# From head 16 on, two pieces of a pair's attention scores stand back to back on TensorE

## The chip, the core and the metric

The kernel runs on one core of a Trainium2 chip. The metric is the time of one execution in device microseconds (us); a measured figure is the median over several runs. A trace of one profiled execution stands beside it. The engines are called by the names of the profile: PE is TensorE, DVE is VectorE, ACT is ScalarE, POOL is GpSimd, SP is SyncE, which issues the transfers. PEld is PE's loading of weights. PSUM is the memory with eight banks into which PE writes.

## What is computed

Attention over 8 batches of 8 heads, 576 positions, 64 numbers per head, with a mask in blocks of 64; then a dense layer with a low-rank mixing over positions and two large matrices; then a gated layer. All in 32-bit floats.

```python
scores = scale * np.matmul(q, k.transpose(0, 1, 3, 2))
scores = np.where(mask, scores, -1000000000.0)          # block_i >= block_j
attn = softmax(scores); x = np.matmul(attn, v)          # (8, 576, 512)
...
u = x + (x.transpose(0, 2, 1) @ U @ V).transpose(0, 2, 1)
x = u + np.maximum(u @ w_ch1, 0.0) @ w_ch2
...
out = (sigmoid(conv(x, conv_w)) * (x @ w_val)) @ w_out
```

## The kernel before

The 8 x 576 positions are cut into nine groups of 512. For each group and each of 16 slices of the large layer, `emit_h1` sums twelve matmuls into one PSUM bank (tile `h1`, written at line 833; the trace calls it `h`), ACT makes `hh` of it and DVE makes `hl` (lines 861, 862), and `emit_o` adds twelve matmuls to the four accumulators `acc` (line 885). This is the main stream on PE. The accumulators hold four of the eight PSUM banks for the whole time.

The attention of later heads is woven into that stream. `attention` is a generator; `gap()` is called in the middle and at the end of every `emit_h1` and `emit_o`, and pulls about one step of the generator each time. So a step of the attention falls in one of four kinds of place: in the middle of an `h1` sum, after it, in the middle of an `o` sum, after it. In `tick(n, ...)`, four steps of head n come first, i = 0 to 3. From head 16 on (`n >= NQ`), an even head does the scores of itself and the next head there: `emit_s_piece(n // 2, i)` computes piece i of both, one head in each half of PE's rows, into two fresh PSUM banks (tiles `pS`, matmuls at line 381), and ACT copies the two banks out (line 386). Piece 0 has three blocks of 64, 192 and 256 columns per head, piece 1 one of 320, piece 2 one of 448, piece 3 one of 320. [...] There are 24 pairs of heads from head 16 on.

The two `pS` tiles of a piece, `h1`, and the tiles `pPV` (attention times values, line 604), `pT`, `pG` and `pH` (mixing) all come from one pool of four banks, `ps_p`. A bank is free again when its last reader is done: for `h1` that is `hl` on DVE, for `pS` the copy on ACT, for `pPV` the copy `lt` on ACT (line 606).

PE's order is written out by hand: its instructions stand as the code emits them. The order of the other engines is set by a scheduler when the program is built, so it can move when PE's order does.

Of the kernel before, what the change touches and what calls it, by code (L numbers as in the profile page):

```python
# [22 lines left out]
def attn_moe_gate_kernel(ctx: ExitStack, tc: tile.TileContext, q, k, v, U, V, w1, w2, wval, convw, wout, out):  # L23
# [303 lines left out]
    def load_v(n):  # L327
        if not 0 <= n < NH:
            return
        vv = v[n // H, n % H]  # L330
        t = vstk[n % 2]
        sp.dma_start(out=t[:, 0:NK - 1, 0:D], in_=vv[0:S - D, :].rearrange("(i p) d -> p i d", p=P))
        sp.dma_start(out=t[D:P, NK - 1, 0:D], in_=vv[S - D:S, :])
# [4 lines left out]
    def spare(nm, n):  # L338
        return st_p.tile([P, n], F32, tag=nm, name=nm)
# [4 lines left out]
    def prep_t(pn):  # L344
        if pn >= B * NP:
            return
        t = raw.pop(pn)
        if 2 * pn < NQ:
            tq = rot("tk" if pn % 2 else "tq", 1)
            z = kz[pn % 2]  # L350
            for rows in own if pn == 0 else (slice(0, P),):
                vec.transpose(tq[rows], t["q"][rows])
                for a in range(2):
                    if pn or rows == own[a]:
                        vec.transpose(z[own[a], a, :], t["k"][own[a]])
            qkt[pn] = (tq, z)
        else:
            tq, tk = rot("tq", 1), rot("tk", 1)
            vec.transpose(tq, t["q"])
            vec.transpose(tk, t["k"])  # L360
            qkt[pn] = (tq, tk)
        load_qk(pn + 1)

    def kslice(j):
        return slice(q0[j], q0[j] + P) if q0[j] + P <= S else slice(S - P, S)
# [3 lines left out]
    def emit_s_piece(pn, i):  # L369

        heads = (2 * pn, 2 * pn + 1)
        tq, tk = qkt[pn]
        if i == 0:
            for n in heads:
                stt[n] = [spare(("za", "zb")[h], w) if n % 3 == 1 else s_p.tile([P, w], F32, tag=f"s{h}", name=f"s{h}") for h, w in enumerate(sw)]
        ps = [psum["a"].tile([P, 512], F32, tag="a", name="pS") for _ in own]
        o = 0
        for j, a0, a1 in pieces[i]:
            w = a1 - a0
            for t, me in zip(ps, own):  # L380
                pe.matmul(t[:, o:o + w], tk[me, kslice(j)], tq[me, a0:a1], start=True, stop=True)  # L381
            o += w
        j, a0, a1 = pieces[i][0]
        d = soff[j] + a0 - q0[j]
        for n, t in zip(heads, ps):
            act.copy(stt[n][half_of[j]][:, d:d + o], t[:, 0:o])  # L386
# [72 lines left out]
    def emit_corners(n):  # L459
        for h, js in enumerate(((3, 0), (1, 2))):  # L460
            c0, c1 = (soff[j] // D for j in js)
            v_ = stt[n][h].rearrange("p (c w) -> p c w", w=D)
            pool.memset(v_[D:P, c0:c1 + 1:c1 - c0, :], MASKED)
        pool.memset(sv(n, NK - 1)[0:D], MASKED)
# [7 lines left out]
    def emit_max_a(n):  # L472
        m = rot("m", 1)
        vec.tensor_tensor(m[:, P:], sv(n, 0, P), sv(n, 1), op=ALU.max)
        for j in range(2, NK):
            x = vec.tensor_tensor(m[:, q0[j]:], m[:, q0[j]:], sv(n, j), op=ALU.max)
        noted(1, x)
        mxt[n] = m

    def emit_max_b(n):  # L480
        m = mxt.pop(n)
        t = rot("t")
        vec.transpose(t[:, 0:P], sv(n, 0)[:, 0:P])
        vec.transpose(t[:, P:], m[:, P:])
        r = tiny_p.tile([P, NB32], F32, tag="r0", name="r0")
        vec.reduce_max(r, t.rearrange("p (j a) -> p j a", a=32), axis=AX.X)
        mxt[n] = r

    def emit_max_c(n):
        r = mxt.pop(n)  # L490
        r2 = tiny_p.tile([P, NB32], F32, tag="r1", name="r1")
        vec.tensor_copy(r2[0:64], r[64:128])
        yield
        vec.tensor_tensor(r[0:64], r[0:64], r2[0:64], op=ALU.max)
        yield
        vec.tensor_copy(r2[0:32], r[32:64])
        yield
        vec.tensor_tensor(r[0:32], r[0:32], r2[0:32], op=ALU.max)
        yield
        vec.tensor_copy(r[32:64], r[0:32])  # L500
        yield
        vec.tensor_copy(r[64:128], r[0:64])
        yield
        mb = rot("mb", 1)
        vec.transpose(mb.rearrange("p (j a) -> p j a", a=32), r.rearrange("p (j o) -> p j o", o=1).to_broadcast([P, NB32, 32]))
        mbt[n] = mb


    def emit_sub(n, half):
        mb = mbt[n]  # L510
        for j in parts[half]:
            noted(3, vec.tensor_tensor(sv(n, j), sv(n, j), mb[:, q0[j]:], op=ALU.subtract))  # L512
# [3 lines left out]
    def prep_v(n):  # L516

        if not FIRST_SPLIT <= n < NH:
            return
        t = vstk[n % 2]  # L520
        vlo[n] = late["v"].tile([P, NK, D], F32R, tag="vlo", name="vlo")
        if not vhi:
            vhi[0] = late["v"].tile([P, NK, P], F32R, tag="vhi", name="vhi")
            act.copy(vhi[0][:, :, D:P], t[:, :, D:P])
        v_, h_ = t[:, :, 0:D], vhi[0][:, :, 0:D]
        hi_act(h_, v_)
        lo(pool, vlo[n], v_, h_)
# [3 lines left out]
    def emit_exp(n):  # L531
        if n < FIRST_SPLIT:
            return
        for half in range(2):
            s = stt[n][half][:, 0 if half else WHOLE:]
            act.activation(s, s, AF.Exp, scale=scale)  # L536
# [73 lines left out]
    def emit_norm_a(pn):  # L610
        lt = lts.pop(pn)
        t = rot("t")
        with behind(NR0 if pn < NP else 0):
            vec.transpose(t, lt)
        r = tiny_p.tile([P, NB32], F32, tag="r0", name="r0")
        vec.tensor_scalar(r, t.rearrange("p (j a) -> p j a", a=32)[:, :, 0], 1e-9, None, op0=ALU.add)
        vec.reciprocal(r, r)
        nrm[pn] = r

    def emit_norm_b(pn):  # L620
        xt, r = xts[pn], nrm.pop(pn)
        rb = rot("t")
        vec.transpose(rb.rearrange("p (j a) -> p j a", a=32), r.rearrange("p (j o) -> p j o", o=1).to_broadcast([P, NB32, 32]))
        pool.tensor_tensor(xt, xt, rb, op=ALU.mult)
# [90 lines left out]
    def tick(n, mixed, last=B * NP):  # L715


        e = n - DEPTH
        new, old = n < NH, 0 <= e < NH

        load_v(e + 1)
        for i in range(4):
            if n < NQ:
                with tc.high_priority():
                    emit_q_bank(n, i)
            elif new and n % 2 == 0:
                emit_s_piece(n // 2, i)
            if i == (0 if n % 2 else 3) and new and n >= NQ:
                emit_corners(n)
                emit_max_a(n)  # L730
            yield
        if new:
            if n >= NQ:
                emit_max_b(n)
            if n % 2 == 1:
                prep_t((n + 1) // 2)
        yield from mixing(2 * e, mixed, last)
        if new and n >= NQ:
            for _ in emit_max_c(n):
                pass  # L740
            emit_sub(n, 0)
            emit_sub(n, 1)
        if old:
            emit_pv(e, 0)
            yield
        if new and n >= NQ:
            emit_exp(n)
        if old:
            emit_pv(e, 1)
        prep_v(e + 1)  # L750
        emit_est(e + 1)
        if old:
            if e % 2 == 1:
                with tc.high_priority() if URG and e == H - 1 else ExitStack():
                    emit_norm_a(e // 2)
                    emit_norm_b(e // 2)
            yield
        yield from mixing(2 * e + 1, mixed, last)

    def mixing(at, first, last=B * NP):  # L760

        for step, delay in ((mix_H2, H0), (mix_G, G0), (mix_T, T0)) if last == NP else ((mix_H2, HPOS), (mix_G, GPOS), (mix_T, TPOS)):
            pn, off = divmod(at - delay, 4)
            if off == 0 and first <= pn < last:
                if URG and pn == NP - 1:
                    with tc.high_priority():
                        for _ in step(pn):
                            pass
                else:
                    yield from step(pn)  # L770
                yield step is mix_H2 and pn % NP == NP - 1
# [391 lines left out]
```

## Time and profile before

| | |
|---|---|
| median of 3 runs | 1480.73 us (1478.81 to 1481.48) |
| span of the profiled execution, first to last instruction | 1473.3 us |
| PE busy / ACT busy / DVE busy | 1426.3 us (97%) / 718.5 us (49%) / 1054.8 us (72%) |
| chain that ended last, PE's share | 82% |
| matmuls of the score pieces (line 381) | 576 rows, from 218.6 to 1005.6 us |

A busy engine is one with an instruction in it; matmuls overlap, so PE's pace is read from the distance between the starts of two matmuls, not from their durations. The profiled span and the measured median differ by 7.4 us; that part lies around the span and has no instructions of the kernel.

### The profile page before, as it was taken

What the parts mean: (1) busy time and instruction counts of PE and PEld (TensorE: products, weight loads), DVE (VectorE), ACT (ScalarE), POOL (GpSimd) and SP (SyncE); (2) the same over time, 40 slices, a digit from 0 to 9 for tenths busy, and PEclk for the clock granted to TensorE, in tenths of its full rate; (3) what the DMA queues carried; (4) which work ended last, traced back from release to release, by engine and by line L of the source; (5) the groups of instructions that cost most, each with busy time, mean ns of one, the idle gap of its engine ahead of it and who ended that gap; (6) DMA issues with size and microseconds to landing.
All of it is one profiled execution on the core that took longest, in us unless ns stands there. A gap on an engine that the chain in (4) does not pass through costs nothing.

```text
span 1473.3 us, 20082 instructions
## 1 busy us (share of the span) xinstructions
PE 1426.3 (97%) x6706; PEld 1102.3 (75%) x6706; DVE 1054.8 (72%) x2224; ACT 718.5 (49%) x1529; POOL 297.8 (20%) x420
## 2 busy tenths in 40 slices
PE   6888899899999999999999999999999999999999
PEld 3656666677777777777777777777888888788887
DVE  7878877967786888777778878777224326399991
ACT  4676564555555546565555555555322221344332
POOL 2113332212121112112211211121122100343310
PEclk9999999999999999999999999999999999999999
DMA  6445764543343434333434433332255433223311
GB/s 123 104 106 154 217 210 130 152 110 96 84 102 110 95 96 111 96 86 82 124 82 111 114 83 96 96 95 70 86 159 167 147 128 123 92 72 101 109 56 65
DMA packets 246288, 163.56 MB, mean 111 GB/s; under 512 B 197669, under 2 KB 212261, under 8 KB 246186
## 3 DMA queue, kind: packets, MB, share of 16 engines
q1 hardware_dynamic: 246186, 162.29, 39.6%
q8 instruction: 53, 0.87, 0.3%
q14 instruction: 49, 0.40, 0.1%
HBM read 134.98 MB, written 27.26 MB: 110 GB/s over the span
## 4 chain that ended last, share of the span: by engine, by line
PE 82%; DVE 10%; DMA 3%; ACT 2%; issue 1%; SPq 1%; POOL 0%; DVEq 0%; ACTq 0%
PE acc L885 25%; PE h L833 25%; PE pPV L604 8%; PE o L999 7%; PE val L975 6%; PE pS L381 6%; DMA raw<-in_moe_w_ch_dram 1%; DVE wa L123 1%; DVE rq L425 1%; PE pG L680 1%; PE acc L878 1%; PE pS L416 1%; DVE wa L141 1%; PE pT L664 1%; DVE wa L120 1%
## 5 line engine op out<-in xcount | busy, mean ns | idle before, releaser
L885 PE MATMUL acc<-hh,w 128*128 128x512 f32 x1152 | 401.0, 402 | 0.0
L885 PEld LDWEIGHTS acc<-hh,w 128*128 128x128 f32 x1152 | 217.1, 188 | 67.6 <-issue 22.5
L833 PE MATMUL h<-uh,w1hi 128*128 128x512 f32 x576 | 238.5, 414 | 2.3 <-ACT lt L606 1.2
L833 PE MATMUL h<-uh,w1lo 128*128 128x512 f32 x576 | 226.4, 393 | 0.0
L885 PE MATMUL acc<-hl,w 128*128 128x512 f32 x576 | 225.9, 392 | 0.0
L833 PE MATMUL h<-ul,w1hi 128*128 128x512 f32 x576 | 225.7, 392 | 0.0
L862 DVE SCALAR_TENSOR_TENSOR hl<-h,hh 128x512 fp32r<-128x512 f32 x144 | 98.5, 684 | 143.2 <-ACT hh L861 142.0
L861 ACT ACTIVATE hh<-h 128x512 fp32r<-128x512 f32 x144 | 85.9, 596 | 173.9 <-PE h L833 167.9
L833 PEld LDWEIGHTS h<-uh,w1hi 128*128 128x128 f32 x576 | 108.6, 189 | 45.7 <-issue 20.4
L95 POOL TENSOR_TENSOR vlo<-vstk,vhi 128x320 fp32r<-128x320 f32 x46 | 43.0, 934 | 455.3 <-ACT vhi L89 389.2
L833 PEld LDWEIGHTS h<-uh,w1lo 128*128 128x128 f32 x576 | 108.4, 188 | 24.2
L885 PEld LDWEIGHTS acc<-hl,w 128*128 128x128 f32 x576 | 108.8, 189 | 19.8 <-issue 0.7
L833 PEld LDWEIGHTS h<-ul,w1hi 128*128 128x128 f32 x576 | 108.7, 189 | 19.6 <-issue 1.3
L957 DVE SCALAR_TENSOR_TENSOR gt<-yb,cw,gt 128x516 f32<-128x516 f32 (+1 forms) x144 | 115.2, 830 | 1.4
L381 PE MATMUL pS<-tq,tk 64*128 64x320 f32 (+4 forms) x576 | 96.7, 429 | 1.5 <-DVE hl L862 0.8
L95 POOL TENSOR_TENSOR yl<-yb,yh 128x512 fp32r<-128x512 f32 (+7 forms) x64 | 66.9, 1078 | 107.4 <-ACT yh L89 107.3
L386 ACT COPY s<-pS 128x320 f32<-128x320 f32 (+2 forms) x128 | 60.2, 497 | 48.7 <-PE pS L381 47.5
L95 POOL TENSOR_TENSOR ul<-xt,uh 128x512 fp32r<-128x512 f32 (+7 forms) x64 | 53.8, 850 | 108.0 <-ACT uh L89 107.9
L536 ACT ACTIVATE s<-s 128x448 f32<-128x448 f32 (+1 forms) x62 | 44.0, 710 | 64.8 <-DVE s L512 64.8
L381 PEld LDWEIGHTS pS<-tq,tk 64*128 64x128 f32 x576 | 43.8, 185 | 37.8 <-issue 22.2
L512 DVE TENSOR_TENSOR s<-s,mb 128x64 f32<-128x64 f32 (+4 forms) x160 | 68.7, 493 | 0.3
L605 ACT COPY xt<-pPV 64x128 f32<-64x128 f32 (+1 forms) x128 | 50.1, 391 | 25.8 <-PE pPV L604 23.9
(169 smaller groups left out, 2758.8 us busy)
## 6 DMA issues: line engine op xcount, KB each, us to landing
w<-w_s SPq DMA_DIRECT2D x144, 512.0 KB, 3.3
rawq<-in_q_dram SPq DMA_DIRECT2D x128, 72.0 KB, 2.8
rawk<-in_k_dram SPq DMA_DIRECT2D x128, 72.0 KB, 3.1
out_dram<-ot SPq DMA_DIRECT2D x35, 256.0 KB, 2.0
vstk<-in_v_dram SPq DMA_DIRECT2D x64, 128.0 KB, 2.7
raw<-in_moe_w_ch_dram SPq DMA_DIRECT2D x64, 128.0 KB, 2.8
raw<-in_moe_w_ch_dram SPq DMA_DIRECT2D x16, 512.0 KB, 3.9
w_s<-wo SPq DMA_DIRECT2D x16, 512.0 KB, 3.3
```

Of the source, the lines that this page charges most:

```text
L95: eng.tensor_tensor(o, i, f32(h), op=ALU.subtract)
L381: pe.matmul(t[:, o:o + w], tk[me, kslice(j)], tq[me, a0:a1], start=True, stop=True)
L386: act.copy(stt[n][half_of[j]][:, d:d + o], t[:, 0:o])
L512: noted(3, vec.tensor_tensor(sv(n, j), sv(n, j), mb[:, q0[j]:], op=ALU.subtract))
L604: pe.matmul(o_, l_, r_, start=(i == 0), stop=(i == len(todo) - 1))
L833: pe.matmul(ps[:, 0:n], w[:, d, fs], x[:, d, 0:n], start=(d == 0 and i == 0), stop=(d == ND - 1 and i == 2))
L861: act.activation(hh[:, 0:n], ps[:, 0:n], AF.Relu)
L862: latest[0] = vec.scalar_tensor_tensor(hl[:, 0:n], ps[:, 0:n], 0.0, f32(hh[:, 0:n]), op0=ALU.max, op1=ALU.subtract)
L885: pe.matmul(acc[d][:, 0:n], w[:, wi, ds], x[:, 0:n], start=False, stop=(f == NF - 1 and i == 2))
L957: vec.scalar_tensor_tensor(gt[d][:, 0:gw], y[:, d, j:j + gw], cw[:, d, j:j + 1], gt[d][:, 0:gw], op0=ALU.mult, op1=ALU.add)
L975: pe.matmul(ps[:, 0:n], w[:, d, es], x[:, d, 0:n], start=(i == 0), stop=(i == 3 * ND - 1))
L999: pe.matmul(ps[:m, cs], x[:, e, a:a + m], w[:, e, cs], start=(i == 0), stop=(i == 3 * ND - 1))
```

## The change

Two lines in `tick`. Steps i = 0 and i = 2 now emit two pieces each, steps 1 and 3 none; the yields stay, so nothing else moves to another step.

```diff
-            elif new and n % 2 == 0:
+            elif new and n % 2 == 0 and i % 2 == 0:
                 emit_s_piece(n // 2, i)
+                emit_s_piece(n // 2, i + 1)
```

On PE in the middle of an `h1` sum, before (the last block of piece 0, half of the sum, piece 1; `w` and `u` names are weights and inputs, numbers are buffers; the bracket names the engines waited for):

```order
L381 MATMUL pS_4344<-tq_4244,tk_4245 128x256
L381 MATMUL pS_4345<-tq_4244,tk_4245 128x256
L833 MATMUL h1_4331<-uh_757,w1hi_148 128x512
L833 MATMUL h1_4331<-ul_758,w1hi_148 128x512
L833 MATMUL h1_4331<-uh_757,w1lo_149 128x512
L833 MATMUL h1_4331<-uh_757,w1hi_148 128x512
L833 MATMUL h1_4331<-ul_758,w1hi_148 128x512
L833 MATMUL h1_4331<-uh_757,w1lo_149 128x512
L381 MATMUL pS_4364<-tq_4244,tk_4245 128x320 [waits PE_49,Activation_49]
L381 MATMUL pS_4365<-tq_4244,tk_4245 128x320 [waits Activation_49]
```

The same place now (lines below 727 of the new file stand one further down):

```order
L381 MATMUL pS_4344<-tq_4244,tk_4245 128x256
L381 MATMUL pS_4345<-tq_4244,tk_4245 128x256
L381 MATMUL pS_4354<-tq_4244,tk_4245 128x320 [waits PE_49,Activation_49]
L381 MATMUL pS_4355<-tq_4244,tk_4245 128x320 [waits Activation_49]
L834 MATMUL h1_4331<-uh_757,w1hi_148 128x512
L834 MATMUL h1_4331<-ul_758,w1hi_148 128x512
L834 MATMUL h1_4331<-uh_757,w1lo_149 128x512
```

Piece 1 moved ahead of the second half of the sum. `h1` holds a bank here; the built program gives the four `pS` tiles banks 6, 7, 4 and 6 again.

On PE after an `h1` sum, before (end of piece 0, half of an `o` sum, piece 1):

```order
L381 MATMUL pS_4023<-tq_3918,tk_3919 128x256
L885 MATMUL acc0_3225<-hh_3895,w2_3899 128x512 [waits DMAHW4_49]
L885 MATMUL acc0_3225<-hl_3896,w2_3899 128x512
L885 MATMUL acc0_3225<-hh_3895,w2_3899 128x512
L885 MATMUL acc1_3226<-hh_3895,w2_3899 128x512
L885 MATMUL acc1_3226<-hl_3896,w2_3899 128x512
L885 MATMUL acc1_3226<-hh_3895,w2_3899 128x512
L381 MATMUL pS_4040<-tq_3918,tk_3919 128x320 [waits PE_49,Activation_49]
L381 MATMUL pS_4041<-tq_3918,tk_3919 128x320 [waits Activation_49]
```

And now:

```order
L381 MATMUL pS_4023<-tq_3918,tk_3919 128x256
L381 MATMUL pS_4032<-tq_3918,tk_3919 128x320 [waits PE_49,Activation_49]
L381 MATMUL pS_4033<-tq_3918,tk_3919 128x320 [waits DVE_49]
L886 MATMUL acc0_3225<-hh_3895,w2_3899 128x512 [waits DMAHW4_49]
L886 MATMUL acc0_3225<-hl_3896,w2_3899 128x512
```

The fourth tile now takes the bank of the sum just finished and waits for DVE's `hl`.

On ACT at one of the six places where a group of positions ends, before (copies of `pPV`, casts `eh`, exponentials at lines 536 and 556):

```order
L89 CAST eh_7287<-za_6768 128x448
L89 CAST eh_7291<-zb_6769 128x768
L556 ACTIVATE ef_7285<-za_6768 128x384
L605 COPY xt_7260<-pPV_7268 64x448
L606 COPY lt_7261<-pPV_7268 64x448
L89 CAST vhi_2942<-vstk1_153 128x5x64
L536 ACTIVATE s0_7088<-s0_7088 128x448
L536 ACTIVATE s1_7089<-s1_7089 128x768
```

And now:

```order
L89 CAST eh_7287<-za_6768 128x448
L536 ACTIVATE s0_7088<-s0_7088 128x448
L89 CAST eh_7291<-zb_6769 128x768
L556 ACTIVATE ef_7285<-za_6768 128x384
L536 ACTIVATE s1_7089<-s1_7089 128x768
L605 COPY xt_7260<-pPV_7268 64x448
L606 COPY lt_7261<-pPV_7268 64x448
```

Both exponentials of line 536 moved ahead of the copies `xt` and `lt`; the next `pT` (line 672) waits for `lt`.

## Rows read from the trace of the kernel before

**Rows 1.** Windows: stretch, its length, then busy us by engine, granted clock, DMA.

```profile
300.00:1012.00 712.00, 711.08 (x3500) 547.35 (x3499) 555.83 (x1234) 392.16 (x833) 129.93 (x237) 1.00 0.38 98
```

**Rows 2.** Waits of PE, 300 to 1012 us: total, times, longest.

```profile
PE pT L672 <- ACT lt L606: 0.9, 2, 0.7
```

**Rows 3.** Timeline of PE (start, length, instruction, count): pieces 0 and 1 apart.

```profile
425.22 0.39 PE L833 MATMUL h<-uh,w1lo 128*128 128x512 f32 x1
425.54 1.25 PE L381 MATMUL pS<-tq,tk 64*128 64x64 f32 x12
426.72 0.50 PE L833 MATMUL h<-uh,w1hi 128*128 128x512 f32 x1
427.06 0.40 PE L833 MATMUL h<-ul,w1hi 128*128 128x512 f32 x1
...
428.01 0.39 PE L833 MATMUL h<-uh,w1lo 128*128 128x512 f32 x1
428.32 0.81 PE L381 MATMUL pS<-tq,tk 64*128 64x320 f32 x4
429.06 0.50 PE L885 MATMUL acc<-hh,w 128*128 128x512 f32 x1
429.40 0.39 PE L885 MATMUL acc<-hl,w 128*128 128x512 f32 x1
429.63 0.62 PE L885 MATMUL acc<-hh,w 128*128 128x512 f32 x2
```

**Rows 4.** Timeline of PEld, weight loads in the same stretch.

```profile
426.72 0.19 PEld L833 LDWEIGHTS h<-uh,w1hi 128*128 128x128 f32 x1 [0.33 <-issue]
...
427.06 0.19 PEld L833 LDWEIGHTS h<-uh,w1lo 128*128 128x128 f32 x1
```

**Rows 5.** Timelines where pieces 0 and 1 already adjoin: PE, PEld, DVE, ACT.

```profile
292.56 2.28 PE L381 MATMUL pS<-tq,tk 64*128 64x64 f32 x16
294.77 0.50 PE L885 MATMUL acc<-hh,w 128*128 128x512 f32 x1
...
293.43 0.64 PE L381 MATMUL pS<-tq,tk 64*128 64x256 f32 x3
293.64 0.70 PE L381 MATMUL pS<-tq,tk 64*128 64x320 f32 x2
294.04 0.29 PEld L381 LDWEIGHTS pS<-tq,tk 64*128 64x128 f32 x2 [0.21 <-DVE hl L862]
293.29 0.69 DVE L862 SCALAR_TENSOR_TENSOR hl<-h,hh 128x512 fp32r<-128x512 f32 x1
293.84 1.73 ACT L386 COPY s<-pS 128x512 f32<-128x512 f32 x4 [0.58 <-PE pS L381]
```

**Rows 6.** ACT by form, 300 to 1012 us: busy us, mean ns, idle before.

```profile
L536 ACT ACTIVATE s<-s 128x768 f32<-128x768 f32 x28 | 23.6, 842 | 4.6 <-DVE s L512 4.6
L536 ACT ACTIVATE s<-s 128x448 f32<-128x448 f32 x28 | 16.2, 579 | 52.2 <-DVE s L512 52.2
L386 ACT COPY s<-pS 128x512 f32<-128x512 f32 x28 | 15.8, 591 | 1.9 <-PE pS L381 1.7
```

**Rows 7.** Timelines of PE and DVE, first and last of five places after `h1`.

```profile
393.82 1.25 PE L381 MATMUL pS<-tq,tk 64*128 64x64 f32 x12
396.60 1.25 PE L381 MATMUL pS<-tq,tk 64*128 64x320 f32 x4
396.81 0.68 DVE L862 SCALAR_TENSOR_TENSOR hl<-h,hh 128x512 fp32r<-128x512 f32 x1
...
927.00 1.25 PE L381 MATMUL pS<-tq,tk 64*128 64x64 f32 x12
929.29 0.68 DVE L862 SCALAR_TENSOR_TENSOR hl<-h,hh 128x512 fp32r<-128x512 f32 x1
```

**Rows 8.** Windows on either side of a fall of PE's clock.

```profile
284.00:287.10 3.10, 1.24 (x5) 0.66 (x4) 2.97 (x9) 2.28 (x6) 0.00 (x0) 0.99 0.53 169
287.10:290.50 3.40, 3.40 (x9) 2.40 (x8) 3.30 (x10) 2.54 (x7) 0.00 (x0) 0.50 0.00 0
```

## The prediction

> **What bounds the kernel now.** I read the busy shares by stage first. In the stretch that holds most of the changed places, 300 to 1012 us, PE has an instruction in it for 711.08 of 712 us at the full granted clock, while DVE and ACT are busy 556 and 392 us [rows 1]. The table of waits for the same stretch has one line for PE, 0.9 us in all [rows 2]. So PE sets the time of this stage, it hardly waits by that view, and whatever lengthens or shortens PE's row of matmuls there goes into the end one to one, until PE begins to wait. The timeline then shows what a piece of scores costs PE. In the plain stream, matmuls of 512 columns start 0.23 us apart (429.40 to 429.63). Around piece 0 three distances are longer: 0.32 from the last `h` matmul to the piece, 1.18 from the piece's start to the next `h` matmul, 0.34 from that one to the second [rows 3].
>
> **What a changeover costs.** From 425.22 to 427.06 are 1.84 us, of which two plain steps are 0.46, so piece 0 costs 1.38. Piece 1, 428.01 to 429.40, is 1.39, less 0.46: 0.93. Apart, the two cost 2.31 [rows 3]. There is one place before the change where a step of the generator was drawn twice and the two adjoin: there piece 1 begins 1.08 after piece 0 (292.56 to 293.64), and its second head begins late, at 294.04, because it waited for `hl` [rows 5]. From that late start to the next stream matmul (294.77) are 0.73, as long as a piece 1 that stands alone (0.74). With a lateness L of the second head an adjoining pair thus costs 0.32 + 1.08 + L + 0.74 + 0.34 - 0.46 = 2.02 + L. Against 2.31 it saves 0.29 - L. Without any lateness the second head runs beside the first with no changeover of its own; what that is worth more is the slower first step after a changeover, 0.34 - 0.23 = 0.11 [rows 3]. So a free junction saves 0.40, and one whose fourth tile is late costs L - 0.29. At the one place in the trace L was 0.39 (294.04 against 293.65), so it lost 0.10.
>
> The trace also says why a changeover costs: inside the stream the weights of the next matmul are loaded from the moment the one before starts (load and earlier matmul both at 427.06, the load 0.19 long); after a piece the load starts only with its own matmul, at 426.72 [rows 3, 4]. The Trainium skill, page "TensorE: Matmul & The Clock Gate", Part 3 on packing small matmuls, says that a weight load overlaps matmuls in flight only where the row groups differ. Taken at its word, every matmul of the stream would carry its load and a junction would save nothing in particular; the 0.23 steps speak against it. What that would make of the sum is a rival below.
>
> **The change part by part.** No instruction is added or removed: PE has the same matmuls, ACT the same copies, SP the same transfers. 24 pairs of heads give 48 places, one of which adjoins already, so 47 are new. In the order, the places of pieces 0 and 2 stay; pieces 1 and 3 move up by one step. What decides is the pool of four banks, which four tiles use up at once. By what stands before and after them on PE, the 47 fall in three kinds.
>
> *18 places where the fourth tile takes the bank of the pair's own first tile*: the 12 in the middle of an `h1` sum (the sum holds one bank, three are free) and 6 after a sum with pieces 2 and 3. The chain can be read at the joined place: piece 0's last matmul starts at 293.43, ACT's first copy at 293.84, 0.41 later; the copy is 0.59 [rows 5, 6]; from the end of a releaser to PE's load are 0.06 (`hl` ends 293.98, load 294.04 [rows 5]). So the bank is free 1.06 after 293.43, at 294.49, and the tile is due at 293.65: L = 0.84. Each costs 0.84 - 0.29 = 0.55, together +9.9. Bounds 0.65 to 1.0 for L, since pieces 2 and 3 copy fewer columns and ACT may be busy: +6.5 to +12.8.
>
> *5 places after a sum with pieces 0 and 1*: the fourth tile takes the finished sum's bank and waits for `hl`. In the first, the tile is due at 393.82 + 1.09 = 394.91, and `hl` ends at 397.49, plus 0.06: L = 2.64. In the last, due 928.09, free 930.03: L = 1.94 [rows 7]. `hl` stands behind a backlog on ACT and DVE that does not move with PE; PE itself comes later, having lost about 0.55 at the place before. I take L = 1.8, bounds 1.3 to 2.6. Before, PE waited here too: piece 1 at 396.60 should take 0.74, and with 396.60 to 397.79 it took 1.19, so 0.45 go there; as the other places lie between that and nothing, I take 0.2. Each costs 1.8 - 0.29 - 0.2 = 1.3, together +6.5 (bounds +4 to +10.5). Behind the waiting tile stands the whole stream; nothing on PE passes it.
>
> *24 places about an `o` sum* (13 in its middle, 11 after it): `h1` was read out long ago and four banks are free. 24 x 0.40 = -9.6. After an `o` sum, though, the next `h1` is a fifth tile and takes the first tile's bank: free 0.84 after piece 1's start, due after 0.63 to 0.74: 0.1 to 0.2 late, 11 x 0.15 = +1.7. Together -7.9.
>
> *ACT's order.* The scheduler moves the exponentials of line 536 at the six places where a group of positions ends: one of 0.84 or two, 0.84 + 0.58 = 1.42 [rows 6], now stand ahead of the copy `lt` for which `pT` on PE waits. In two of these places PE waited for `lt` already, so there is no slack in them [rows 2]; in the others the slack is not known. Nothing to 1.42 each; I take 1.0, near the single one: +6.0, bounds 0 to +8.5. A gain is excluded, since nothing moved ahead of `xt` or `lt` leaves. The other moves (`hh` behind the pair's copies instead of between them) I cost at nothing: a sum of `h1` is read out while the `o` half-sums run; without that cover it would be 0.59 per copy in front of it, which is part of the bounds for `hl`.
>
> The sum: +9.9 + 6.5 - 7.9 + 6.0 = +14.5 us. The profiled span of 1473.3 becomes 1487.8; the same added to the median of 1480.73, which stands 7.4 above the span, gives 1495.2.
>
> **The rivals.**
>
> A, faster: the fourth tile is not late at the 18 places, because its bank comes free in time. Each then saves 0.40 instead of costing 0.55: -17.1, sum -2.6; with `lt` early as well, -8.6, time 1472. It decides at L = 0.29 for those places: the copy would have to end 0.55 sooner, so a copy of 0.59 would have to be nearly gone. The copy's row speaks against it. 0.05.
>
> B, no change: L is 0.65 and 1.3 at the two kinds of late places and ACT's order costs nothing, because PE, itself late, finds `lt` done. +6.5 + 4 - 7.9 = +2.6, time 1483.3. For it: four of the six places show no wait for `lt` now. Against it: it needs all low ends at once. 0.14.
>
> C, dearer by the clock: after a stretch in which PE was busy only 1.24 of 3.10 us its granted clock was 0.50, the level of 1.2 GHz, for 3.4 us [rows 8]; half of 3.4 is 1.7 us lost at most. The five waits for `hl` are new gaps of up to 2.6 us. Five such falls make +8.5, sum +23, time 1503.7. Against it: PE still runs the third tile for part of each gap. The same page of the Trainium skill, Part 1 on the clock gate, says that the low level is the default and that activity releases the high one; rows 8 agree. 0.12.
>
> D, junctions save nothing, every load being as dear as another: 24 x 0.40 is lost from the sum and 0.29 at the 23 others, +14.5 + 9.6 + 6.7 = +30.8, time 1511.5. The 0.23 steps against a load of 0.19 [rows 3, 4] speak against it. The weight-load rule named above gives this. 0.03.
>
> That the change does not do what it says is excluded by the order: 47 junctions are there.
>
> **How the numbers follow.** The forecast, 1495, has 0.66, A 0.05, B 0.14, C 0.12, D 0.03. The low ends of the terms give +2.6, the high ends 12.8 + 10.5 - 7.9 + 8.5 = +23.9; both at once are unlikely, and B and C lie near the ends. The range is 1484 to 1506 and leaves out A, D and half of B and of the tail above. 0.2% is 3 us, about what a measurement of this kernel can tell from no change: faster 0.06, within 0.2% 0.12, slower 0.82.
>
> **What would show it.** Right, if the table of waits of the new kernel between 215 and 1030 us names `pS` waiting for ACT's copy, 18 times for some 0.8 us less what runs beside, `pS` waiting for `hl` five times for over 1 us, and `pT` waiting for `lt` about six times; if free junctions take 0.4 less in the timeline; and if PE's other distances stay. It is wrong in its first step if junctions in the middle of an `o` sum save much more or less than 0.40, in its second if the fourth tile at a sum's middle starts under 0.3 late, in its last if `pT` waits no longer than now. A granted clock of 0.50 in this stage would speak for C.

## The result and the profile after

The changed kernel takes 1489.84 us (median of 4 runs, 1487.82 to 1490.66) against 1480.73: a ratio of 1.0076 with a 95% interval of 1.0061 to 1.0091. In a second series of runs (f1_after_again), where the kernel before takes 1475.59, it takes 1488.83: ratio 1.0096 (1.0083 to 1.0110). Forecast were 1495.2, and slower.

| | before | after |
|---|---|---|
| span of the profiled execution | 1473.3 us | 1486.0 us |
| PE busy / ACT busy / DVE busy | 1426.3 / 718.5 / 1054.8 us | 1425.5 / 718.1 / 1045.1 us |
| chain that ended last: PE, DVE, ACT | 82%, 10%, 2% | 78%, 11%, 5% |

PE and ACT are busy for as long as before; what grew is waiting. From the windows of after, the stretch that answers to [rows 1], and PE's waits there (us in total, times, longest), then the waits of PEld, the loading of weights:

```profile
300.00:1025.00 725.00, 710.79 (x3498) 558.49 (x3497) 544.72 (x1237) 390.94 (x832) 127.28 (x235) 1.00 0.37 96
```

```profile
PE pT L672 <- ACT lt L606: 7.5, 6, 1.9
PE pS L381 <- DVE hl L863: 3.5, 5, 0.7
PE acc L886 <- DVE hl L863: 0.2, 1, 0.2
```

```profile
PEld pS L381 <- ACT s L386: 6.7, 11, 0.6
PEld pS L381 <- DVE hl L863: 6.1, 5, 1.2
...
PEld pS L381 <- ACT zb L386: 1.8, 3, 0.6
PEld pS L381 <- ACT za L386: 1.3, 2, 0.6
```

PE had 711.08 of 712 us busy [rows 1] and has 710.79 of 725 now. Six waits of `pT` and five of `pS` for `hl` stand in PE's own table. The waits for the copy of the pair's own first tile are not there, since PE is still running the third tile for nearly all of each; they are 11 + 3 + 2 = 16 lines of the weight loads, as many as there are such places in this stretch.

A measure that does not depend on where a run started is used from here on, the **stage**: from the first to the last of the 46 matmuls `pH` between 296 and 1022 us. Of before and of after (times min/median/max, then first and last start):

```profile
L703 PE MATMUL pH<-vst,g x46: 192/280/368, 301.1 to 1007.5; 128*128 128x128 f32 x8, 128*128 128x384 f32 x8, 128*128 128x192 f32 x8, 128*128 128x320 f32 x8
```

```profile
L703 PE MATMUL pH<-vst,g x46: 192/278/367, 300.1 to 1020.2; 128*128 128x128 f32 x8, 128*128 128x384 f32 x8, 128*128 128x192 f32 x8, 128*128 128x320 f32 x8
```

The stage took 706.4 and takes 720.1: 13.7 longer. In the trace of the second series it takes 721.7 (298.9 to 1020.6). So two traces of one kernel differ by 1.6 us here; a fall of PE's clock inside the stage makes it, as is shown under the rivals. Ahead of the stage the executions differ by several us whatever the kernel, so the stage is the sharper measure. Of before there is one trace.

**A free junction** (pieces 2 and 3 in the middle of an `o` sum), PE's timeline of after:

```profile
430.78 0.39 PE L886 MATMUL acc<-hh,w 128*128 128x512 f32 x1
431.10 1.56 PE L381 MATMUL pS<-tq,tk 64*128 64x448 f32 x8
432.59 0.50 PE L886 MATMUL acc<-hh,w 128*128 128x512 f32 x1
432.93 0.40 PE L886 MATMUL acc<-hl,w 128*128 128x512 f32 x1
```

Each matmul of the program is two rows here, so these two pieces of one block for two heads are 8 rows, and pieces 0 and 1 below are 16. From the last matmul of the sum to the second one behind are 2.15 us. Apart the two pieces take 1.61 + 1.39 - 0.46 = 2.54 in the same count (pieces 0 and 1: 1.84 + 1.39 - 0.46 = 2.77 by [rows 3]). So 0.39 is saved.

**A junction that waits for its own first tile** (pieces 0 and 1 in the middle of an `h1` sum), PE, PEld and ACT of after:

```profile
425.18 0.39 PE L834 MATMUL h<-uh,w1lo 128*128 128x512 f32 x1
425.50 2.72 PE L381 MATMUL pS<-tq,tk 64*128 64x64 f32 x16
428.15 0.50 PE L834 MATMUL h<-uh,w1hi 128*128 128x512 f32 x1
428.49 0.39 PE L834 MATMUL h<-ul,w1hi 128*128 128x512 f32 x1
...
427.42 0.29 PEld L381 LDWEIGHTS pS<-tq,tk 64*128 64x128 f32 x2 [0.65 <-ACT za L386]
426.78 0.59 ACT L386 COPY za<-pS 128x512 f32<-128x512 f32 x1 [0.41 <-PE pS L381]
```

The chain of the prediction can be read off. Piece 0's last matmul starts 0.87 behind the junction's begin (292.56 to 293.43 in [rows 5]), here at 426.37; ACT's copy follows 0.41 later, takes 0.59 and ends at 427.37, and the fourth tile's weights are loaded at 427.42. The tile was due 1.09 behind the junction's begin, at 426.59, so it is 0.83 late. The bracket at the copy says that ACT was idle until then and waited for PE. The distance is 3.31 instead of 2.77: 0.54 lost.

**A junction that waits for `hl`**, PE, ACT and DVE of after:

```profile
393.13 0.39 PE L834 MATMUL h<-uh,w1lo 128*128 128x512 f32 x1
393.45 1.78 PE L381 MATMUL pS<-tq,tk 64*128 64x64 f32 x14
395.94 0.80 PE L381 MATMUL pS<-tq,tk 64*128 64x320 f32 x2 [0.71 <-DVE hl L863]
396.67 0.50 PE L886 MATMUL acc<-hh,w 128*128 128x512 f32 x1
397.01 0.39 PE L886 MATMUL acc<-hl,w 128*128 128x512 f32 x1
...
394.34 0.60 ACT L862 ACTIVATE hh<-h 128x512 fp32r<-128x512 f32 x1
395.21 0.68 DVE L863 SCALAR_TENSOR_TENSOR hl<-h,hh 128x512 fp32r<-128x512 f32 x1
```

The distance is 3.88 instead of 2.77: 1.11 lost. The tile was due at 394.54 and starts at 395.94, 1.40 late.

**`pT` behind `lt`** at the end of a group, PE and ACT of after:

```profile
449.81 0.40 PE L834 MATMUL h<-uh,w1lo 128*128 128x512 f32 x1
451.17 0.30 PE L672 MATMUL pT<-ident,xt 128*64 128x128 f32 x1 [0.96 <-ACT lt L606]
...
447.57 0.58 ACT L536 ACTIVATE za<-za 128x448 f32<-128x448 f32 x1
448.77 0.85 ACT L536 ACTIVATE zb<-zb 128x768 f32<-128x768 f32 x1
450.58 0.53 ACT L606 COPY lt<-pPV 64x448 f32<-64x448 f32 x1
```

The exponentials stand ahead of `lt`, and PE is idle for 0.96 here.

By kind, in the 42 junctions inside the stage (the same to 0.01 at each place of a kind): 16 that wait for their own tile 0.48 to 0.54, together +8.1; 5 that wait for `hl` 1.11, together +5.55, of which PE waited about 1.0 in before too; 10 free ones in the middle of `o` -0.40 or -0.39 each, 11 after `o` -0.20 or -0.25, together -6.4; and the six waits of `pT`, 7.5 less the 0.9 of [rows 2]. 8.1 + 4.5 - 6.4 + 6.6 = 12.8 of the 13.7.

### The profile page after: what moved, and what is told of

Read it like the earlier page. It is cut to its first block, busy times and chain, and to the rows that moved or that the text cites. A ratio compares the mean times of both kernels' runs of the same rounds, so it can differ in the third digit from the quotient of the medians.

```text
span 1486.0 us, 20104 instructions
## 1 busy us (share of the span) xinstructions
PE 1425.5 (96%) x6706; PEld 1115.3 (75%) x6706; DVE 1045.1 (70%) x2224; ACT 718.1 (48%) x1529; POOL 296.9 (20%) x420
## 4 chain that ended last, share of the span: by engine, by line
PE 78%; DVE 11%; ACT 5%; DMA 3%; issue 1%; SPq 1%; POOL 0%; DVEq 0%; ACTq 0%
PE acc L886 24%; PE h L834 23%; PE pPV L604 8%; PE o L1000 7%; PE val L976 6%; PE pS L381 4%; DMA raw<-in_moe_w_ch_dram 2%; DVE wa L123 1%; PE pG L680 1%; DVE rq L425 1%; PE acc L879 1%; DVE wa L141 1%; ACT lt L606 1%; PE pS L416 1%; PE pT L664 1%
## 5 line engine op out<-in xcount | busy, mean ns | idle before, releaser
L381 PE MATMUL pS<-tq,tk 64*128 64x320 f32 (+4 forms) x576 | 100.9, 416 | 9.1 <-DVE hl L863 5.0
L381 PEld LDWEIGHTS pS<-tq,tk 64*128 64x128 f32 x576 | 53.4, 186 | 49.5 <-issue 24.5
L95 DVE TENSOR_TENSOR el<-s,eh 128x448 fp32r<-128x448 f32 (+1 forms) x62 | 46.6, 788 | 28.3 <-PE pPV L604 16.8
```

What stands on the lines that cost most here:

```text
L95: eng.tensor_tensor(o, i, f32(h), op=ALU.subtract)
```

## Experiments

These are three series on three chips, each beside runs of the kernel before on the same chip, where that takes 1474.20 us (e1, e2, e5, e7), 1474.95 (e9, e10, e3, e4) or 1475.59 (the others). The last column sets one trace against the one trace of before.

| kernel | ratio to before (95%) | stage, us | against 706.4 |
|---|---|---|---|
| changed kernel again | 1.0096 (1.0083 to 1.0110) | 721.7 | +15.3 |
| e1_free | 1.0041 (1.0027 to 1.0054) | 712.7 | +6.3 |
| e2_late | 1.0106 (1.0090 to 1.0122) | 721.2 | +14.8 |
| e12_mid_h1 | 1.0058 (1.0042 to 1.0073) | 713.6 | +7.2 |
| e5_order | 1.0087 (1.0074 to 1.0100) | 717.5 | +11.1 |
| e7_free_order | 1.0019 (1.0007 to 1.0032) | 708.7 | +2.3 |
| e9_after_hh | 1.0042 (1.0029 to 1.0055) | 712.2 | +5.8 |
| e10_free_hh | 0.9964 (0.9953 to 0.9975) | 703.0 | -3.4 |
| e11_before_hh | 0.9993 (0.9981 to 1.0005) | 705.0 | -1.4 |
| e3_five_apart | 0.9977 (0.9966 to 0.9988) | 703.5 | -2.9 |
| e4_five_joined | 0.9872 (0.9853 to 0.9892) | 687.0 | -19.4 |

Of the changed kernel run again a stage 13 to 14 us longer and a ratio of 1.0075 to 1.009 had been expected; both came out a little higher, the stage by the fall of the clock named above.

### The two halves of the change

`at[0]` says in which sum a step is drawn; the free half takes "o", the late half "h".

```diff
...
             elif new and n % 2 == 0:
-                emit_s_piece(n // 2, i)
+                if i % 2 == 0:
+                    both = at[0] == "o"
+                    emit_s_piece(n // 2, i)
+                    if both:
+                        emit_s_piece(n // 2, i + 1)
+                elif not both:
+                    emit_s_piece(n // 2, i)
...
```

> The kernel before, in which only those pieces adjoin that are drawn about an o sum (24 places, where the traces show four free banks); at all other places the pieces stay apart, except the one place in which the kernel before had them adjoining already. Theory (banks): each free junction saves 0.40 in the middle of a sum and about 0.2 after one, as the trace of the changed kernel shows (13 x 0.40 + 11 x 0.22 = 7.6 saved). But ACT's order moves here as it does in the changed kernel: the exponentials of line 536 stand ahead of the copy lt at six places, which in the changed kernel's trace cost 7.1. So -7.6 + 7.1 = -0.5: 1480, no difference, with pT waiting for lt some 7 us in all. Rival (ACT's order is not on the path; pT's wait replaces another that would come anyway): -7.6, 1473. Rival (every junction costs the same, 9.1 / 47 = 0.19 each): 24 x 0.19 = +4.6, 1485.

> The other half: only those pieces adjoin that are drawn about an h1 sum (23 places of the changed kernel and the one that adjoined before). ACT's exponentials stay behind lt here, as in the kernel before. Theory (banks): 18 places whose fourth tile waits for the copy of the pair's own first tile, +0.53 each by the changed kernel's trace = +9.6; 5 places that wait for hl, +0.9 each = +4.5, perhaps up to the 6.5 of the prediction; together +14 to +16: 1495 to 1497, slower than the changed kernel although it joins half as many pieces. Rival (every junction costs the same 0.19): 23 x 0.19 = +4.4, 1485. Rival (ACT's order made the loss of the changed kernel and the junctions nothing): 1481.

Measured: +6.4 us by the medians (1480.64 against 1474.20) for the free half and +15.8 (1490.04) for the late half. The late half falls where the theory put it and far from an equal cost per junction: half as many junctions lose as much as all of them. The free half lost, where the theory had nothing. Its junctions do save (-4.5 in its trace's stage), but its waits of PE from 300 us on are:

```profile
PE pT L672 <- ACT lt L606: 8.1, 6, 2.2
PE acc L895 <- DVE hl L871: 0.2, 1, 0.2
```

The six waits for `lt` are here, and in the late half they are not (1.1 us in 3). So it is the free junctions that move the exponentials in the scheduler's order, not the late ones. I had the wait right at 7 and the junctions too large at 7.6: in this kernel the five free junctions of pieces 0 and 1 in the middle of an `o` sum save 0.12 in all, where those of the changed kernel save 2.00. In its stage, -4.5 from the junctions, +7.2 from `pT`'s waits (8.1 less 0.9) and about 1.6 from a fall of PE's clock behind the longest of them (from 317 us on) make 4.3 of the 6.3; the other 2 are not accounted for. One of the five in the later kernel e10_free_hh, which has the same junctions, PEld and ACT:

```profile
365.03 0.29 PEld L381 LDWEIGHTS pS<-tq,tk 64*128 64x128 f32 x2 [0.32 <-ACT lt L606]
364.45 0.53 ACT L606 COPY lt<-pPV 64x448 f32<-64x448 f32 x1
```

There PE comes earlier than ACT is done with the bank of `pPV`. In the changed kernel `lt` ends at 362.54 at this place, and the tile is due at 363.24, so the bank is free. This goes not with how late PE is but with pieces 2 and 3 of the pair of heads before. Where these adjoined, ACT's last exponentials end 2.9 to 3.3 us ahead of the next pair's piece 0, and `lt` ends 0.4 behind its start; where they stood apart, it is 0.7 to 2.0 ahead and 0.7 to 1.6 behind. This holds without exception at the 15 places per trace where pieces 0 and 1 stand in the middle of an `h1` sum, after it, or in the middle of an `o` sum, in eight traces (before, after, e1, e2, e5, e9, e10, e12). A likely mechanism is that the pair's last scores come a step earlier on PE when the pieces adjoin, and with them the subtractions on DVE and the exponentials on ACT. No edit tried this by itself.

### Only the middle of an h1 sum

As the late half, with `at[0]` set to another value ahead of the last `gap()` of `emit_h1`.

> Only the 12 places in the middle of an h1 sum adjoin (and the one that did before); ACT's exponentials stay behind lt. It measures the wait for the copy of the pair's own first tile by itself. Theory: 12 x 0.53 = +6.4 us by the changed kernel's distances, 12 x 0.55 = 6.6 by the prediction: ratio 1.0043 to 1.0045. Rival (the half that joins about h1 sums lost its 15 us to hl alone, at the places after a sum): ratio 1.000 or below.

Measured +7.1 (1482.68 against 1475.59), ratio 1.0058, a little over the 6.4 to 6.6. The wait for the own copy is real without `hl`. Its size is not constant: pieces 2 and 3 lose 0.50 each at five places in the stage, pieces 0 and 1 lose 0.94 to 1.27 instead of 0.54 at five others. That is 7.8 in all; PE's waits for `hl` in before, 1.07, are gone, and `pT` waits 0.6 longer, which makes 7.3 of the stage's 7.2. Ten places at 0.53 would be 5.3, so the nearness to 6.4 is in part luck. ACT's timeline says why (the junction starts on PE at 427.27):

```profile
428.26 0.53 ACT L606 COPY lt<-pPV 64x448 f32<-64x448 f32 x1
428.81 0.46 ACT L89 CAST vhi<-vstk 128x320 fp32r<-128x320 f32 x1
429.29 0.58 ACT L386 COPY za<-pS 128x512 f32<-128x512 f32 x1
```

The copy waits for ACT, which still has `lt` and `vhi` to do. In the changed kernel ACT was idle when its copy could start. There pieces 2 and 3 of the pair before adjoin, and here they stand apart. PE's lateness is not what decides: in e2_late, which has them apart too, the junction starts at 425.48, in after at 425.50, and the last two exponentials ahead of it begin on ACT at 422.90 in the one and at 420.02 in the other.

### ACT's order given back

```diff
...
-        if new and n >= NQ:
-            emit_exp(n)
         if old:
             emit_pv(e, 1)
+        if new and n >= NQ:
+            with tc.issue_after(lt_copy[0]) if old and e % 2 == 0 else nullcontext():
+                emit_exp(n)
...
```

`lt_copy[0]` holds the newest copy `lt`.

> The changed kernel with ACT's order as in the kernel before at the six places: the exponentials of line 536 are emitted and issued behind the copy lt. PE's order is untouched. Theory: the six waits of pT for lt (7.5 us in the changed kernel's table of waits, 7.1 by the distances) shrink to what they were before, under 1.5 in all: 1489.8 - 6.5 = 1483.3. Rival (order not on the path): no difference, 1489.8. Rival (given back: the exponentials come later, and the next head's products wait for them instead): between, 1486 to 1490, with pPV or h waiting for ACT.

> Both at once: only the 24 free junctions about an o sum, and ACT's order kept as before at the six places. Theory: -7.6 and nothing against it: 1473, faster than both kernels by 0.5% and 1.1%. Rival (junctions save nothing, the changed kernel's gain at the o sums comes from somewhere else): 1481. Rival (every junction costs 0.19): 1485.

In PE's order nothing moved, and on ACT only the twelve exponentials of the six places (on DVE two pairs of neighbours changed places). Yet the changed kernel gained little (ratio 1.0087 against 1.0096, the intervals overlap), and the free half stayed slower than before (1475.98 us, where 1473 was expected). In e5_order `pT`'s wait is gone and another has come. PE's waits from 300 us on, then DVE and PE at one place:

```profile
PE acc L888 <- DVE hl L865: 3.6, 4, 1.4
PE pS L381 <- DVE hl L865: 3.6, 5, 0.7
PE pT L673 <- ACT lt L606: 0.8, 1, 0.8
```

```profile
723.69 2.78 DVE L512 TENSOR_TENSOR s<-s,mb 128x64 f32<-128x64 f32 x5
726.40 0.68 DVE L865 SCALAR_TENSOR_TENSOR hl<-h,hh 128x512 fp32r<-128x512 f32 x1
727.13 0.50 PE L888 MATMUL acc<-hl,w 128*128 128x512 f32 x1 [1.25 <-DVE hl L865]
```

The exponentials now delay `hh`, but `hh` is done 1.7 to 2.2 us before `hl` starts at the three longest of these waits. What holds `hl` are the five subtractions (2.78 us) ahead of it on DVE; they stand there in the changed kernel too, where `pT`'s wait hid them. e7_free_order has the same wait, 4.2 us in 5. So the time is given back, as the second rival of e5_order's expectation has it (1486 to 1490; measured 1487.29), but by `acc` waiting for DVE, which it does not name. The next edit puts the exponentials behind `hh` as well: `emit_exp` is called after the following `yield`, inside `tc.issue_after` of the newest `hh`.

> The changed kernel once more with the exponentials of line 536 taken out of lt's way, but now behind the next sum's hh as well, which in the run before had been held up by them (PE waited 4.6 us for hl in its new place). PE's order is untouched. Theory: from 296 us on the changed kernel loses 13.3 us by its distances, 7.1 of them at pT; without pT's waits and without new ones for hl about 6 are left: about 6 to 7 us faster than the changed kernel, 0.3 to 0.4% slower than before. Rival (given back once more: the casts of pT's copies stand behind the exponentials now, and pG waits for them): as slow as the changed kernel, with pG or h waiting. Rival (junctions and not the order carry pT's wait): pT still waits 7 us for lt.

> Only the 24 free junctions about an o sum, with the exponentials behind lt and hh. With them ahead of lt this kernel was 0.4% slower than before, although its junctions each saved 0.20 to 0.41 in the trace (4.7 us from 296 on), because pT and pG together lost 11 us; with them behind lt but ahead of hh it was 0.2% slower. Theory: the 4.7 and what lies before 296 us stay, nothing stands against them: 0.2 to 0.5% faster than before. Rival (a wait for another engine appears wherever PE comes earlier, since DVE and ACT have no slack there): within 0.1% of before.

> The kernel before, its pieces apart, with nothing but the exponentials of line 536 held behind lt and hh. It tells whether the gain of the kernel with the 24 free junctions (ratio 0.9964) came from the junctions or from this order. Theory: PE waited 0.9 us for lt in the kernel before, so up to 0.9 us, 0.06%: ratio 0.999 to 1.001. Rival (the order alone made the gain): 0.996 to 0.997.

With that, the changed kernel's stage loses 5.8 instead of 13.7 to 15.3, and the free half is faster than both kernels: 1470.11 us, ratio 0.9964 (0.9953 to 0.9975). The order alone gives 0.9993, not distinguishable from 1, so the gain needs the junctions. The stages of these two, 703.0 and 705.0, differ by 2.0, less than half of the about 4.4 that the junctions save in e10's trace; 1.4 of the rest are waits for `lt` that e11_before_hh does not have. With `hh` earlier, the scheduler also puts `hl` ahead of the subtractions, as DVE of e9_after_hh shows:

```profile
719.89 0.65 DVE L866 SCALAR_TENSOR_TENSOR hl<-h,hh 128x512 fp32r<-128x512 f32 x1
720.47 2.08 DVE L512 TENSOR_TENSOR s<-s,mb 128x64 f32<-128x64 f32 x5
```

PE's waits from 300 us on in e10_free_hh:

```profile
PE pT L672 <- ACT lt L606: 1.4, 2, 1.0
PE acc L898 <- DVE hl L874: 0.2, 1, 0.2
```

Two edits are in this order, the place on ACT and what it does to DVE's order; which of them carries more was not tried.

### A fifth bank

```diff
...
-    ABUF = 4
+    ABUF = 5
...
-            accs[g] = [psum["acc"].tile([P, GS], F32, tag=f"acc{d}", name=f"acc{d}") for d in range(ND)]
+            accs[g] = [psum["acc"].tile([P, GS], F32, tag=f"acc{d}", name=f"acc{d}") for d in range(ND - 1)]
+            accs[g].append(accs[g][-1])
...
```

The fifth bank for scores is taken from the accumulators: the last two quarters of the columns of the second large product are summed into one bank, so that both kernels leave out these columns' proper output. Both also hold the exponentials behind `lt` and `hh`.

> The kernel before with five banks in the pool of scores instead of four. The fifth is taken from the accumulators: the last two quarters of the columns of the large layer's second product share one bank and are summed together, so the output of these columns is not the reference's; the number and kinds of instructions on PE are the same. The early stage has one bank less, so only the difference to the next kernel is read. The exponentials stand behind lt and hh in both. No theory has a number for its distance to before; the theory of the banks has 0 from 296 us on to within 2 us, since apart no tile waits for a bank now.

> The changed kernel with the same five banks, so that a fourth tile never has to take a bank of its own pair or of the sum just finished. Like the kernel above it sums the last two quarters of the columns into one bank. Theory of the banks: all 47 junctions are free now, 0.40 in the middle of a sum and 0.20 after one: 25 x 0.40 + 22 x 0.20 = 14 us faster than the kernel above, the same edit that with four banks made it 9 us slower. Rival (the score matmuls of two pieces in a row are slower by themselves, or ACT can't copy eight tiles in a row in time): within 3 us of the kernel above, or slower. Rival (PE coming earlier is given back to hl and lt): between, 4 to 8 us faster.

Measured 1471.94 and 1456.37: joining is 15.6 us faster with five banks. With four banks and the same order of the exponentials it is slower (e9_after_hh against e11_before_hh: stage 712.2 against 705.0, +7.2). The stages, 703.5 and 687.0 (to the same 46th `pH`), differ by 16.5. All 42 junctions are alike now: 21 of pieces 0 and 1 take 2.37, 21 of pieces 2 and 3 take 2.15, 0.40 and 0.39 less than apart, and 21 x 0.79 = 16.6. The place in the middle of an `h1` sum that lost 0.54 above, PE's timeline of e4_five_joined, and all of its waits from 300 us on:

```profile
418.50 0.39 PE L837 MATMUL h<-uh,w1lo 128*128 128x512 f32 x1
418.82 1.79 PE L381 MATMUL pS<-tq,tk 64*128 64x64 f32 x16
420.54 0.50 PE L837 MATMUL h<-uh,w1hi 128*128 128x512 f32 x1
420.87 0.39 PE L837 MATMUL h<-ul,w1hi 128*128 128x512 f32 x1
```

```profile
PE acc L890 <- DVE hl L866: 0.2, 1, 0.2
```

With a bank to spare no junction loses anything. The expectation of 14 was low because it gave the junctions after a sum only 0.20; with a fifth bank these save 0.40 too. The Trainium skill, page "Perfetto Trace Analysis", section "Matmuls", says that independent groups of matmuls should rotate through different banks, so that the copy of one runs beside the matmuls of the next. The two pairs of runs agree: with as many banks as tiles in flight a loss of about 7 us becomes a gain of 16.

## Why the prediction was right, point by point

**Bound and direction.** PE sets the stage, and what PE loses goes into the end one to one: the stage grew by 13.7, it began 1.0 earlier, and behind it both traces take the same 465.8 us, so the span grew by 12.7. The sum was +14.5. Right in sign, and 1489.84 lies in the range, 5.4 below the forecast; in the second series the median grew by 13.2.

**The changeover.** 0.40 for a free junction was right to 0.01 in the middle of an `o` sum, and its 0.25 after one measured 0.20 to 0.25. It holds at all 42 places with a fifth bank. That speaks against D: by the page "TensorE: Matmul & The Clock Gate" of the Trainium skill, Part 3, taken at its word, these would save nothing. That all ten places in the middle of an `o` sum save 0.40 here is in part luck: in e1_free, where ACT has a backlog, five of them save 0.12 in all.

**The 18 places.** 0.55 each was put, 0.48 to 0.54 measured, which is a lateness of 0.77 to 0.83 (the loss and 0.29) instead of 0.84. The step holds, but is less general than it read: ACT has to be idle when the piece ends. With a backlog it is 0.94 to 1.27 (e12_mid_h1). In the changed kernel ACT has none at these places, and that goes with pieces 2 and 3 of the pair before, which adjoin there; the prediction had no such effect of one junction on the next.

**The five places with `hl`.** Mis-sized: a lateness of 1.8 was taken from rows of before that gave 2.64 and 1.94 [rows 7]. It is 1.40 (1.11 and 0.29), the same at all five. The prediction's reason was a backlog on ACT and DVE that stays where it is while PE comes later. In after that backlog is gone: the exponentials that stood in front (ACT, 391.14 and 392.14 us in before) start at 388.56, and ACT and DVE are idle here until PE's own products `pPV` come:

```profile
391.48 0.83 ACT L89 CAST eh<-s 128x768 fp32r<-128x768 f32 x1 [0.28 <-PE pPV L604]
392.25 1.49 DVE L95 TENSOR_TENSOR el<-s,eh 128x448 fp32r<-128x448 f32 x2 [1.20 <-PE pPV L604]
```

So 1.40 is what is left of the way from PE over ACT and DVE back to PE, and it moves with PE; it is the same in e2_late, e5_order and e9_after_hh. The term is 4.5 instead of 6.5.

**ACT's order.** 6.0 was put and 6.6 measured, six waits as named. What was not seen: it is no term of the change as a whole but hangs on the free junctions, so that the half meant as a pure gain pays for it and is slower than before by itself. Nor was it seen that moving the exponentials back does not simply return the time, because `hl` on DVE was late by nearly as much.

**Rivals.** A is out, since the 16 places in the stage are all late. B needed every term at its low end, tiles late by 0.65 and 1.3 and nothing from ACT's order; measured were 0.77 to 0.83, 1.40 and 6.6 us. C is real in one of two traces, for one fall and not five, and behind another wait than it named. In the trace of after the clock falls ahead of the stage, from 263 us on, behind the junction at 257.5 where PE waited 2.3 us for a copy:

```profile
263.00:266.50 3.50, 3.50 (x10) 2.69 (x9) 3.50 (x8) 1.11 (x2) 1.27 (x3) 0.52 0.23 35
```

Before had such a fall of 3.4 us at another place ahead of the stage [rows 8], so it makes little of the difference. In the second series (f1_after_again) there is one inside the stage, behind the last of the six waits for `lt`:

```profile
994.20 0.30 PE L672 MATMUL pT<-ident,xt 128*64 128x128 f32 x1 [1.85 <-ACT lt L606]
990.00:995.40 5.40, 3.54 (x19) 2.63 (x18) 5.20 (x12) 4.96 (x10) 0.81 (x1) 1.00 0.26 76
995.40:998.80 3.40, 3.40 (x10) 2.68 (x9) 3.40 (x8) 2.20 (x5) 0.10 (x1) 0.51 0.00 0
```

At 0.51, the level of 1.2 GHz, eight steps of the stream take 0.42 to 0.43 us instead of 0.23. That is 1.6 us, the whole difference between this stage (721.7) and that of after (720.1). The window from 300 to 1025 us of the same trace still prints a clock of 1.00: one fall does not show in so long a mean. The waits of PE for `hl`, up to 0.7 us, were followed by no fall in either trace.

**What was to be seen.** `pT` six times and `hl` five times were right. That PE's table would name 18 waits for the copy was wrong: a wait that begins while the tile before still runs shows in the weight loads, not in PE. The granted clock of about 0.50 that was to speak for C is there in the second series.

**The base.** This is where most of the 5.4 us between forecast and result lies. The sum was set on a median that stands 7.4 us above the span of the trace, as if those 7.4 lay around every span. In every execution for which the record has both figures, the time is 1.7 to 1.8 us above the span. By that the traced execution of before took about 1475.1 us, an estimate, 5.6 below the median of its three measured runs. The sum on its own base gives 1473.3 + 14.5 + 1.8 = 1489.6, against 1489.84 measured; that these are so near is in part luck, since the span grew by 12.7 and not 14.5, and the traced execution of after lies 2.0 below its median. The median grew by 9.1 us in the first result and by 13.2 in the second series mainly because that of before is 1480.73 in the one and 1475.59 in the other, while those of the changed kernel differ by 1.0; why is open.

## What to carry to other kernels

Before two bursts that fill a pool of banks are put together, count the tiles in flight with the one that other work holds: the first tile over the pool pays the whole way of an older tile, last matmul, wait of the copy, copy, and pays more when the copying engine has a backlog. Such a backlog can depend on how the work of the step before was placed, so a price read at one place need not hold at the next. Where a scheduler orders the other engines, an edit on PE also edits them; compare their order at the places where PE has no slack, and when a wait is taken away, look at the next engine in line before counting it as gained. The edit that pays here is the half with free banks, with the displaced exponentials held behind both `lt` and `hh`.

## What the runs showed of the hardware

Two changeovers between the matmuls of 64 rows and those of 128 rows cost 0.40 us when the two pieces stand apart, and it does not matter which sum surrounds them (2.37 and 2.15 us at all 42 places of e4_five_joined). I had not expected that a wait for a bank of over half a microsecond leaves hardly any idle time in PE's own rows: at 425.50 us one row of 16 matmuls covers 2.72 us, where 1.79 are enough when nothing waits (e4_five_joined), and the gap inside it, from the third tile's end at 427.28 to the fourth's start at 427.42, is 0.14.
